# Two entries one behind the other in a hand-ordered opening stage, one transfer per unit, and copied-out pieces ahead of each block

One core of a Trainium2 chip. The metric is the device time of one execution in microseconds (us), lower is better. "Span" is the time from the first to the last instruction of one profiled execution, some 2 us less. "Granted clock" is the share of its full speed at which TensorE, the matrix engine, was allowed to run. VectorE and ScalarE work on what TensorE has left in PSUM, the memory that takes its results; POOL and SP here mostly issue transfers.

## The reference, cut to what matters

```python
# x: (8, 3136, 256); filt_r, filt_i: (1569, 256)
X = np.fft.rfft(x, axis=1)
y = np.fft.irfft(X * (filt_r + 1j * filt_i), n=3136, axis=1)   # per entry
h = y.reshape(25088, 256) @ w_in                               # 1024 columns
solu = h * softmax(h)
ln = (solu - mean(solu)) / np.sqrt(var(solu) + 1e-6) * g_ln
out = ln @ w_out
```

The transform over 3136 = 49 x 64 points is done with matrix products. One entry passes through a first stage (`pa`, eight pieces of x, results `t` stored to DRAM as `d`), a spectrum stage (`pb`, products with the filter, `pc`, results `g` stored to DRAM), and a last stage (`py`, results in `y`). Then 196 blocks of 128 rows each compute `h`, the maximum `nmax`, exp, `solu`, its square, a transposition by transfer, and `po`. The transform of the later entries is spread over the blocks of the earlier ones. The opening has nothing to hide behind: entry 0 must be through before the first block.

## The kernel before

PSUM is shared by four pools; `ps_b` has one buffer, which holds `pb` until the products have read it. "Products" are VectorE's three operations `p`, `i` and their sum; the two "turned copies" into `i` that they need are ScalarE's.

```python
GROUPS = [                       # entries, blocks of the first stage, blocks of the spectrum
    ((0, 1), None, None),        # the opening: both entries in every unit
    ((2,), (0, 6), (9, 13)),
    # ... three more groups
]
ps_h = pool("ps_h", 2, PSUM)     # h (and pa, pb in the opening)
ps_b = pool("ps_b", 1, PSUM)     # pb in the blocks
ps_t = pool("ps_t", 2, PSUM)     # pa, pc, py in the blocks
ps_o = pool("ps_o", 1, PSUM)     # po

def multiply(self, i):           # the products of a unit
    # ...
    nc.scalar.mul(turned[0:NQ], ps[NQ:P], -1.0)          # "i": ps is pb
    nc.scalar.copy(out=turned[NQ:P], in_=ps[0:NQ])
    nc.vector.tensor_tensor(out=pt, in0=ps, in1=part(0), op=ALU.mult)      # "p", the last reader of pb
    nc.vector.tensor_tensor(out=turned, in0=turned, in1=part(1), op=ALU.mult)
    nc.vector.tensor_tensor(out=pt, in0=pt, in1=turned, op=ALU.add)

# the blocks: early holds pb, half of pa and half of py; late holds pc, the other halves
with tc.manual_schedule():
    for k in range(blocks + LAG):
        if k < blocks:
            hidden(k)                           # h, nmax, exp
        if 1 <= k <= blocks:
            turn(k - 1)
        if 4 <= k < blocks + 4:
            regroup(*divmod(k - 4, 4))
        for job in early[k]:
            job()
        if k >= LAG:
            po = project(k - LAG)               # po
        if k < blocks:
            normalize(k)                        # solu, square
        if k >= LAG:
            scale(k - LAG, po)
        for job in products[k] + late[k] + stores[k] + loads[k]:
            job()
```

The opening of the kernel before is not ordered by hand; a scheduler places its instructions.

## Time and profile before

| | before |
|---|---|
| time, median of 3 runs (range) | 1904.84 us (1900.58 to 1912.51) |
| span of the profiled run, granted clock | 1902.9 us, 0.968 |
| first `h` begins | 203.42 us |
| from there to the end | 1699.5 us |
| TensorE busy, whole span | 1823.8 us |

### The profile page before, as it was taken

The numbers are of one execution on the slowest core, as the hardware profiler recorded it, in microseconds if no ns is written. First come the engines' busy times: TensorE is split into PE (matmuls) and PEld (weight loads), VectorE is DVE, ScalarE is ACT, GpSimd is POOL, SyncE is SP. The second block draws the span as 40 slices with busy tenths as digits, with TensorE's granted clock in tenths as the row PEclk, the third lists the DMA queues.
The fourth block names the chain that finished last, engine by engine and source line by source line (L and its number), as shares of the span: only waits on it lengthen the run. The fifth ranks groups of instructions, "written<-read, shape, count | busy, mean of one in ns | idle before, by whom it ended". The sixth has DMA issues, their size and how long they took to land.

```text
span 1902.9 us, 21234 instructions
## 1 busy us (share of the span) xinstructions
PE 1823.8 (96%) x6500; PEld 1168.5 (61%) x6500; DVE 1137.0 (60%) x1815; ACT 791.5 (42%) x1297; POOL 440.7 (23%) x1293
## 2 busy tenths in 40 slices
PE   6677889999999999999999999999999999999997
PEld 1224546676666666666666666667677676666665
DVE  1597445567766655566766655566666565566663
ACT  1142344554555544444545434344444334333331
POOL 2010133343334311123333211123322010110110
PEclk9686799999999999999999999999999999999999
DMA  9675279986877866575776656557675545434444
GB/s 268 214 211 188 92 226 239 241 209 174 189 194 204 200 150 149 134 170 140 166 186 148 151 137 141 137 134 177 146 178 112 119 100 117 99 86 110 96 92 100
DMA packets 320399, 300.78 MB, mean 158 GB/s; under 512 B 28625, under 2 KB 286418, under 8 KB 320288
## 3 DMA queue, kind: packets, MB, share of 16 engines
q1 hardware_dynamic: 284624, 206.69, 46.3%
q0 software_dynamic: 26704, 79.63, 14.9%
q10 hardware_dynamic: 8960, 13.11, 2.3%
q8 instruction: 53, 0.87, 0.2%
q14 instruction: 58, 0.48, 0.1%
HBM read 118.44 MB, written 81.40 MB: 105 GB/s over the span
## 4 chain that ended last, share of the span: by engine, by line
PE 88%; DVE 4%; DMA 2%; issue 1%; ACT 1%; POOL 0%; ACTq 0%; DVEq 0%; SPq 0%; POOLq 0%
PE h L396 35%; PE po L456 35%; PE py L253 6%; PE pc L226 4%; PE pb L196 4%; PE pa L169 3%; DMA d<-t 1%; DVE p L217 1%; DVE i L216 0%; DVE p L215 0%; DVE g L229 0%; DMA t<-d 0%; DVE nmax L401 0%; DMA f<-f_dram 0%; DMA raw_in<-in_moe_w_in_dram 0%
## 5 line engine op out<-in xcount | busy, mean ns | idle before, releaser
L456 PE MATMUL po<-w_out_sb,solu_t 128*128 128x256 f32 x3136 | 711.0, 380 | 4.5 <-DVE ot L464 4.5
L396 PE MATMUL h<-w_in_sb,y 128*128 128x512 f32 x1568 | 713.4, 598 | 0.0
L456 PEld LDWEIGHTS po<-w_out_sb,solu_t 128*128 128x128 f32 x3136 | 591.0, 190 | 137.7 <-issue 58.1
L396 PEld LDWEIGHTS h<-w_in_sb,y 128*128 128x128 f32 x1568 | 296.2, 192 | 317.8 <-issue 306.7
L401 DVE TENSOR_REDUCE nmax<-h 128x1 f32<-128x1024 f32 x196 | 239.6, 1222 | 419.6 <-PE h L396 419.6
L404 ACT ACTIVATE e<-h,nmax 128x1024 f32<-128x1024 f32 x196 | 218.5, 1115 | 605.0 <-DVE nmax L401 605.0
L421 ACT ACTIVATE e<-solu,nmu 128x1024 f32<-128x1024 f32 x196 | 225.0, 1148 | 287.9 <-DVE solu L419 287.9
L419 DVE SCALAR_TENSOR_TENSOR solu<-e,rsum,h 128x1024 f32<-128x1024 f32 x196 | 250.9, 1280 | 7.1 <-DVE rsum L416 0.2
L429 DVE STREAM_TRANSPOSE turn<-solu 128x1024 f32<-128x1024 f32 x196 | 241.8, 1234 | 0.0
L235 POOL DMA_DIRECT2D d<-g x152 | 93.7, 621 | 507.5 <-ACT g L229 507.4
L253 PEld LDWEIGHTS py<-wi_t,t 100*128 100x128 f32 x1024 | 146.0, 211 | 51.1 <-issue 36.0
L169 PE MATMUL pa<-x,wf_t 98*100 98x512 f32 x256 | 148.5, 687 | 25.9 <-DMA x<-in_x_dram 12.5
L253 PE MATMUL py<-wi_t,t 100*128 100x98 f32 x1024 | 145.4, 293 | 6.7 <-DMA t<-d 3.5
L448 POOL COPY rs_t<-rs 32x1 f32<-32x1 f32 x784 | 141.7, 181 | 35.7
L464 DVE TENSOR_SCALAR ot<-po,rs_t 128x256 f32<-128x256 f32 x196 | 94.4, 482 | 80.5 <-PE po L456 74.2
L215 DVE TENSOR_TENSOR p<-pb,f 128x512 f32<-128x512 f32 (+1 forms) x101 | 69.0, 684 | 120.4 <-ACT i L208 119.3
L196 PE MATMUL pb<-t,de 128*128 128x512 f32 (+1 forms) x250 | 110.9, 544 | 19.2 <-DVE p L215 10.0
L226 PE MATMUL pc<-p,de 128*128 128x512 f32 (+1 forms) x250 | 110.0, 539 | 14.9 <-DVE p L217 11.5
L442 POOL TENSOR_SCALAR rs<-var 128x4 f32<-128x4 f32 x49 | 9.3, 189 | 445.7 <-ACT e L421 443.6
L169 PEld LDWEIGHTS pa<-x,wf_t 98*100 98x100 f32 x256 | 45.7, 188 | 94.5 <-issue 59.9
L196 PEld LDWEIGHTS pb<-t,de 128*128 128x128 f32 x250 | 47.8, 198 | 78.4 <-issue 43.5
L256 ACT COPY y<-py 128x392 f32<-128x392 f32 x112 | 93.6, 836 | 5.1 <-PE py L253 5.1
(62 smaller groups left out, 868.2 us busy)
## 6 DMA issues: line engine op xcount, KB each, us to landing
solu_t<-turn SPq DMA_DIRECT2D x784, 128.0 KB
t<-d SPq DMA_DIRECT2D x64, 400.0 KB
t<-d SPq DMA_DIRECT2D x198, 128.0 KB
x<-in_x_dram SPq DMA_DIRECT2D x64, 392.0 KB
out_dram<-ot SPq DMA_DIRECT2D x196, 128.0 KB
d<-t POOLq DMA_DIRECT2D x48, 400.0 KB, 5.6
d<-g POOLq DMA_DIRECT2D x148, 128.0 KB, 3.6
f<-f_dram POOLq DMA_DIRECT2D x104, 128.0 KB, 4.3
```

Of the source, the lines that this page charges most:

```text
L169: nc.tensor.matmul(out=ps[0:NK, j], lhsT=wf_t, rhs=self.xs[i][0:NR, 2 * u:2 * u + 2, :], start=True, stop=True)
L196: nc.tensor.matmul(out=ps[:, w * j:w * j + w, :], lhsT=de[:, s + j, 0, :], rhs=t2[:, w * j:w * j + w, :], start=True, stop=True)
L226: nc.tensor.matmul(out=ps[:, w * j:w * j + w, :], lhsT=de[:, s + j, 1, :], rhs=pt[:, w * j:w * j + w, :], start=True, stop=True)
L253: nc.tensor.matmul(out=psv[:, i, :], lhsT=t4s[e, ch][:, i, cb * P:cb * P + P], rhs=wi_t, start=True, stop=True)
L396: nc.tensor.matmul(out=h[:, half, :], lhsT=y[:, c, P * t:P * t + P], rhs=w_in_sb[:, c, 512 * half:512 * half + 512], start=(c == 0), stop= ...
L401: nc.vector.tensor_reduce(out=nmax, in_=h, axis=AX.X, op=ALU.max, negate=True)
L404: nc.scalar.activation(out=e, in_=h, func=AFT.Exp, bias=nmax, accum_out=esum)
L419: nc.vector.scalar_tensor_tensor(out=solu, in0=e, scalar=rsum, in1=hs.pop(k), op0=ALU.mult, op1=ALU.mult, accum_out=nmu)
L421: nc.scalar.activation(out=e, in_=solu, func=AFT.Square, bias=nmu, scale=-float(DFF), accum_out=variances[g][:, i:i + 1])
L429: nc.vector.transpose(out=turns[g][:, :, i, :], in_=solus.pop(k).rearrange("p (f j) -> p f j", j=32))
L448: nc.gpsimd.tensor_copy(out=rss[g][32 * i:32 * i + 32, c:c + 1], in_=rs[32 * c:32 * c + 32, i:i + 1])
L456: nc.tensor.matmul(out=ps, lhsT=solu_t[:, f, :], rhs=w_out_sb[:, f, :], start=(f == 0), stop=(f == KF - 1))
```

## The change

The intent: entries 0 and 1 no longer share units but pass one behind the other, so that entry 1's first stage hides under entry 0's spectrum and entry 0's last stage under entry 1's spectrum. All tables stay resident, a unit's load and store are one transfer each, and the order is fixed by hand. In the blocks, what is copied out of PSUM ("pieces": `pa`, `py`, and with them `pb`) is to stand ahead of `h`, so that its copies run on ScalarE before exp. The core of the diff:

```diff
 GROUPS = [
-    ((0, 1), None, None),
-    ((2,), (0, 6), (9, 13)),
-    ((3, 4), (6, 13), (22, 25)),
+    ((0,), None, None),
+    ((1,), None, None),
+    ((2,), (0, 7), (9, 13)),
+    ((3, 4), (7, 12), (22, 25)),
...
-            for p in range(2):
-                nc.sync.dma_start(out=self.t2s[i][N2 * p:N2 * p + N2, 0:cols, :],
-                                  in_=self.rows(d1[self.n], s, count, p))
+            nc.sync.dma_start(out=self.t2s[i][:, 0:cols, :],
+                              in_=self.columns(d1[self.n], s, count))
...
     with ExitStack() as st:
+        st.enter_context(tc.manual_schedule())
...
+        for sp in sps:
+            if sp.n == 1:
+                for ch in range(4):
+                    fetch_back(0, ch, pools["r"])
+            else:
+                for i in range(3):
+                    sp.fetch(i)
+            forward(sp, 0)
+            for i in range(units):
+                if sp.n == 0 and i in (1, 4):
+                    load_tables(3 + i // 4)
+                sp.multiply(i)
+                if i + 1 < units:
+                    forward(sp, i + 1)
+                if sp.n == 0:
+                    if i < NH // NCH:
+                        first(NH // NCH + i)
+                    if i in (8, 10):
+                        load_weights(i // 2 - 1)
+                elif 2 <= i < 2 + NH // NCH:
+                    for cb in range(KD):
+                        back(0, i - 2, cb, nc.scalar.copy)
+                    ...
+                sp.inverse(i, nc.vector.tensor_copy if sp.n == 0 else nc.scalar.copy)
+                sp.store(i, nc.gpsimd.dma_start)
+                ...
+                if sp.n == 1 and i % 4 == 0 and i < 12:
+                    load_weights(5 + i // 4)
...
     with tc.manual_schedule():
         for k in range(blocks + LAG):
+            for job in early[k]:
+                job()
             if k < blocks:
                 hidden(k)
             if 1 <= k <= blocks:
                 turn(k - 1)
             if 4 <= k < blocks + 4:
                 regroup(*divmod(k - 4, 4))
-            for job in early[k]:
-                job()
+            if k == 1:
+                prepare_w_out()
```

`load_tables` and `load_weights` each issue a transfer and put the VectorE work that needs it right behind it. In the first six blocks both halves of a piece go to `early`.

More of the change, by code (lines that the diff above doesn't have):

```diff
@@ L58, in dft_tables @@
     v[0, :, 0], v[1, :, 0] = 1.0, 0.0
-    wf = np.zeros((N1, 2, 2, NS, 2))
-    wi = np.zeros((2, NS, 2, N1, 2))
+    wf = np.zeros((N1, 2, NS, 2, 2))
+    wi = np.zeros((NS, 2, 2, N1, 2))
     for h in range(2):
-        wf[:, h, :, :, h] = w
-        wi[:, :, h, :, h] = v.transpose(0, 2, 1) / S
+        wf[:, h, :, :, h] = w.transpose(0, 2, 1)
+        wi[:, :, h, :, h] = v.transpose(2, 0, 1) / S
     kap = np.where(q[:, None] < 32, s + N1 * q[:, None], s + N1 * (95 - q[:, None]))
@@ L108 @@
     small = pool("sm", 4)
-    d1 = [dram.tile([len(g[0]), 2 * NS, N2, C], FP32, name=f"d1_{n}") for n, g in enumerate(GROUPS)]
-    d2 = [dram.tile([len(g[0]), 2 * NS, N2, C], FP32, name=f"d2_{n}") for n, g in enumerate(GROUPS)]
+    d1 = [dram.tile([len(g[0]), NS, P, C], FP32, name=f"d1_{n}") for n, g in enumerate(GROUPS)]
+    d2 = [dram.tile([len(g[0]), NS, P, C], FP32, name=f"d2_{n}") for n, g in enumerate(GROUPS)]
     f_dram = dram.tile([NS, NQ, 2, C], FP32, name="f_dram")
@@ L120 @@
     neg_half = consts.tile([P, 4], FP32, name="neg_half")
+    ones = consts.tile([P, P], FP32, name="ones")
+    w_bar = consts.tile([P, C], FP32, name="w_bar")
     nc.vector.memset(neg_half, -0.5)
@@ L148, in __init__, with columns @@
             self.xs, self.t1s, self.t2s, self.fs, self.prods, self.gs = {}, {}, {}, {}, {}, {}
-        def rows(self, ap, s, count, p):
+        def columns(self, ap, s, count):
             if len(self.entries) == 2:
-                return ap[:, p * NS + s, :, :].rearrange("b n c -> n b c")
-            return ap[0, p * NS + s:p * NS + s + count, :, :].rearrange("s n c -> n s c")
+                return ap[:, s, :, :].rearrange("b p c -> p b c")
+            return ap[0, s:s + count, :, :].rearrange("s p c -> p s c")
         def fetch_x(self, i):
@@ L176, in store_first @@
             b, ch = divmod(i, NH // NCH)
-            dma(out=d1[self.n][b].rearrange("a (h n) c -> (a h) n c", h=2)[
+            dma(out=d1[self.n][b].rearrange("s (a n) c -> (s a) n c", a=4)[
                 :, NCH * ch:NCH * ch + NCH, :], in_=self.t1s.pop(i))
@@ L233, in store @@
             gt, cols = self.gs.pop(i), len(self.entries) * count
-            for p in range(2):
-                dma(out=self.rows(d2[self.n], s, count, p),
-                    in_=gt[N2 * p:N2 * p + N2, 0:cols, :])
+            dma(out=self.columns(d2[self.n], s, count), in_=gt[:, 0:cols, :])
     t4s = {}
@@ L245, in fetch_back @@
             out=t4s[e, ch],
-            in_=d2[n][b].rearrange("a (h n) c -> (a h) n c", h=2)[:, NCH * ch:NCH * ch + NCH, :])
+            in_=d2[n][b].rearrange("s (a n) c -> (s a) n c", a=4)[:, NCH * ch:NCH * ch + NCH, :])
     def back(e, ch, cb, evac):
@@ L256, in back, with psum @@
         evac(out=y[:, cb, t0:t0 + S].rearrange("p (r n) -> p n r", n=NH)[:, n0:n0 + NCH, :], in_=psv)
-    flip = [0]
-    def either(out, in_):
-        flip[0] ^= 1
-        if flip[0]:
-            nc.scalar.copy(out=out, in_=in_)
-        else:
-            nc.vector.tensor_copy(out=out, in_=in_)
+    def psum(kind, name):
+        return {"b": ps_b, "t": ps_t, "o": ps_o}[kind].tile([P, 2, C], FP32, name=name, tag=kind)
     with ExitStack() as st:
+        st.enter_context(tc.manual_schedule())
         pools = {name: pool(name + "0", bufs, stack=st)
-                 for name, bufs in (("r", 6), ("t1", 4), ("t2", 5), ("p", 2), ("g", 3))}
-        fpool = pool("fp", 3, stack=st)
+                 for name, bufs in (("r", 5), ("t1", 3), ("t2", 4), ("p", 2), ("g", 3))}
+        fpool = pool("fp", 1, stack=st)
         wpool = pool("wp", 1, stack=st)
+        f_all = fpool.tile([P, NS, 2, C], FP32, name="f_all")
         def load_float64(dst, src, n):
@@ L298, in load_float64, with load_tables @@
             nc.vector.tensor_tensor(out=dst, in0=frac.bitcast(FP32), in1=rest, op=ALU.add)
-        groups = {}
-        def load_group(g):
+        def load_tables(g):
             gs = slice(NG * g, NG * g + NG)
             nc.gpsimd.dma_start(out=de[:, gs, :, :], in_=de_dram[:, gs, :, :])
-            groups[g] = f = fpool.tile([P, NG, 2, C], FP32, name=f"f_{g}", tag="f")
             for k, filt in enumerate((filt_r, filt_i)):
                 for half in range(2):
-                    nc.gpsimd.dma_start(out=f[32 * half:32 * half + 32, :, k, :],
+                    nc.gpsimd.dma_start(out=f_all[32 * half:32 * half + 32, gs, k, :],
@@ L309, in load_group @@
                                         in_=filter_rows(filt, half, NG * g, NG))
-                nc.vector.tensor_copy(out=f[NQ:P, :, k, :], in_=f[0:NQ, :, k, :])
-        def resident(s, count):
-            g, i = divmod(s, NG)
-            if i == 0 and 1 <= g < NS // NG - 2:
-                load_group(g + 2)
-            return groups[g][:, i:i + count]
-        sp = Spectrum(0, pools, resident)
-        for i in range(2 * NH // NCH):
-            sp.fetch_x(i)
-            sp.first(i, (0, 1), ps_h.tile([P, 2, 512], FP32, name=f"pa_0_{i}", tag="h"), either)
-            sp.store_first(i, nc.scalar.dma_start)
-            if i < 3:
-                load_group(i)
@@ L325 @@
-        nc.gpsimd.dma_start(out=wi_t, in_=wi_dram)
-        nc.gpsimd.dma_start(out=g_sb, in_=moe_g_ln.rearrange("(k p) -> p k", p=P))
-        def start(i):
-            sp.fetch(i)
-            sp.fetch_filter(i)
-            sp.forward(i, ps_h.tile([P, 2, 512], FP32, name=f"pb_0_{i}", tag="h").rearrange(
-                "p a (b c) -> p (a b) c", c=C)[:, 0:2, :])
-        start(0)
-        for i in range(NS):
-            sp.multiply(i)
-            if i + 1 < NS:
-                start(i + 1)
-            sp.inverse(i, nc.scalar.copy if i % 3 == 0 else nc.vector.tensor_copy)
-            sp.store(i, nc.scalar.dma_start)
-            if i in (6, 9, 12, 15):
-                c, half = divmod((i - 6) // 3, 2)
-                load_float64(w_in_sb[:, c, 512 * half:512 * half + 512],
-                             w_in_words[P * c:P * c + P, 512 * half:512 * half + 512], f"in{c}{half}")
@@ L345 @@
-        for h in range(4):
-            load_float64(
-                w_out_sb[:, 2 * h:2 * h + 2, :].rearrange("p k d -> p (k d)"),
-                w_out_words[256 * h:256 * h + 256].rearrange("(k p) d w -> p k d w", p=P), f"out{h}")
-        for ch in range(NH // NCH):
-            fetch_back(0, ch, pools["r"])
-            for cb in range(KD):
-                back(0, ch, cb, either)
-        ones = wpool.tile([P, P], FP32, name="ones", tag="ones")
+                nc.vector.tensor_copy(out=f_all[NQ:P, gs, k, :], in_=f_all[0:NQ, gs, k, :])
@@ new lines, in load_weights @@
+        def load_weights(j):
+            if j < 4:
+                c, half = divmod(j, 2)
+                load_float64(w_in_sb[:, c, 512 * half:512 * half + 512],
+                             w_in_words[P * c:P * c + P, 512 * half:512 * half + 512], f"in{j}")
+            else:
+                h = j - 4
+                load_float64(
+                    w_out_sb[:, 2 * h:2 * h + 2, :].rearrange("p k d -> p (k d)"),
+                    w_out_words[256 * h:256 * h + 256].rearrange("(k p) d w -> p k d w", p=P), f"out{h}")
@@ new lines, with first @@
+        sps = [Spectrum(n, pools, lambda s, count: f_all[:, s:s + count]) for n in range(2)]
+        pieces = [(sp, i) for sp in sps for i in range(NH // NCH)]
+        units = len(sps[0].units)
+        def first(n):
+            sp, i = pieces[n]
+            sp.first(i, (0, 1), ps_h.tile([P, 2, 512], FP32, name=f"pa_{sp.n}_{i}", tag="h"),
+                     nc.scalar.copy)
+            sp.store_first(i, nc.scalar.dma_start)
+            if n + 5 < len(pieces):
+                pieces[n + 5][0].fetch_x(pieces[n + 5][1])
@@ new lines, in forward @@
+        def forward(sp, i):
+            sp.fetch_filter(i)
+            sp.forward(i, psum("bo"[i % 2], f"pb_{sp.n}_{i}"))
+        for sp, i in pieces[:5]:
+            sp.fetch_x(i)
+        for n in range(NH // NCH):
+            if n % 3 == 0:
+                load_tables(n // 3)
+            first(n)
+            if n % 3 == 1:
+                load_weights(n // 3)
+            if n == 4:
+                nc.gpsimd.dma_start(out=wi_t, in_=wi_dram)
+                nc.gpsimd.dma_start(out=g_sb, in_=moe_g_ln.rearrange("(k p) -> p k", p=P))
@@ new lines @@
+        for sp in sps:
+            if sp.n == 1:
+                for ch in range(4):
+                    fetch_back(0, ch, pools["r"])
+            else:
+                for i in range(3):
[15 more added lines that the diff above has]
+                        back(0, i - 2, cb, nc.scalar.copy)
+                    if i + 2 < NH // NCH:
+                        fetch_back(0, i + 2, pools["r"])
+                sp.inverse(i, nc.vector.tensor_copy if sp.n == 0 else nc.scalar.copy)
+                sp.store(i, nc.gpsimd.dma_start)
+                if i + 3 < units:
+                    sp.fetch(i + 3)
+                elif sp.n == 0:
+                    sps[1].fetch(i + 3 - units)
+                if sp.n == 1 and i % 4 == 0 and i < 12:
+                    load_weights(5 + i // 4)
@@ L357, with prepare_w_out @@
+    def prepare_w_out():
         nc.vector.memset(ones, 1.0)
@@ L361 @@
                                     op1=ALU.mult)
-        ps = ps_o.tile([P, C], FP32, name="ps_mean", tag="o")
+        ps = psum("o", "ps_mean")[:, 0, :]
         for f in range(KF):
@@ L365 @@
                              start=(f == 0), stop=(f == KF - 1))
-        w_bar = wpool.tile([P, C], FP32, name="w_bar", tag="w_bar")
         nc.scalar.mul(w_bar, ps, 1.0 / DFF)
@@ L452, in project @@
         g, a = divmod(k, 4)
-        ps = ps_o.tile([P, C], FP32, name=f"po_{k}", tag="o")
+        ps = ps_o.tile([P, 2, C], FP32, name=f"po_{k}", tag="o")[:, 0, :]
         solu_t = solu_ts.pop((g, a))
@@ L491 @@
     row_loads = []
-    def psum(kind, name):
-        return (ps_b if kind == "b" else ps_t).tile([P, 2, C], FP32, name=name, tag=kind)
-    for n in range(1, len(GROUPS)):
+    for n in range(2, len(GROUPS)):
         entries, first_at, spectrum_at = GROUPS[n]
@@ L502 @@
             for u in range(2):
-                (early, late)[u][t].append(lambda sp=sp, i=i, u=u: sp.first(
+                (early if t < LAG else (early, late)[u])[t].append(lambda sp=sp, i=i, u=u: sp.first(
                     i, (u,), psum("t", f"pa_{sp.n}_{i}_{u}").rearrange("p a c -> p (a c)").rearrange(
@@ L519 @@
             for cb in range(KD):
-                (early, late)[cb][t].append(
+                (early if t < LAG else (early, late)[cb])[t].append(
                     lambda e=e, ch=ch, cb=cb: back(e, ch, cb, nc.scalar.copy))
```

## The prediction

> **What bounds the kernel now.** I read the page first (busy shares, the 40 slices, the chain), then busy time by stretch, then the timeline of the opening stage, then the groups kept apart by shape.
>
> ```profile
> PE 1823.8 (96%) x6500; PEld 1168.5 (61%) x6500; DVE 1137.0 (60%) x1815; ACT 791.5 (42%) x1297; POOL 440.7 (23%) x1293
> PEclk9686799999999999999999999999999999999999
> DMA  9675279986877866575776656557675545434444
> ```
>
> TensorE is the bound, except in the first five slices or so (47 us each), where neither its clock nor its busy share is full. The table by stretch sharpens this (columns: stretch, length, then PE, PEld, DVE, ACT, POOL busy, granted clock, DMA share, GB/s):
>
> ```profile
> 0.00:50.00 50.00, 33.19 (x44) 9.40 (x44) 9.46 (x11) 6.34 (x6) 12.49 (x24) 0.91 0.92 269
> 50.00:100.00 50.00, 34.06 (x46) 10.88 (x46) 29.75 (x50) 11.82 (x18) 3.39 (x6) 0.65 0.65 212
> 100.00:150.00 50.00, 36.00 (x62) 11.30 (x62) 47.72 (x82) 21.06 (x36) 3.60 (x6) 0.90 0.67 195
> 150.00:200.00 50.00, 38.19 (x136) 29.39 (x137) 30.25 (x60) 10.51 (x15) 2.14 (x3) 0.60 0.49 161
> 700.00:1000.00 300.00, 300.00 (x1116) 196.18 (x1115) 188.16 (x296) 138.00 (x226) 76.32 (x220) 1.00 0.67 159
> ```
>
> 0 to 50 is bound by transfers (92%, 269 GB/s), 100 to 150 by VectorE (47.7 of 50), 150 to 200 by nothing that is full: work follows itself at a low clock. From 350 on TensorE is full. Matmul records at full clock last 0.4325 us for 512 columns (eight of `h` in 3.46 us), 0.216 for 256 (sixteen of `po` in 3.46) and 0.108 for `py` (eight in 0.86). By the counts of the groups: h 1568 x 0.4325 = 678, po 3136 x 0.216 = 678, pa 256 x 0.4325 = 111, py 1024 x 0.108 = 111, pb and pc together 2 x (150 x 0.4325 + 100 x 0.216) = 173; with the mean sum 1754 us. The first `h` stands here:
>
> ```profile
> 203.42 4.98 PE L396 MATMUL h<-w_in_sb,y 128*128 128x512 f32 x6
> ```
>
> Before it lie pa 64 x 0.4325 = 28, pb and pc 100 x 0.4325 = 43, py 128 x 0.108 = 14 and 3 of the mean: 88 us of work in 203 us. The opening loses 115 of the 149 us that the span has above 1754. So the change is judged by when the first block can begin.
>
> **What the Trainium skill says.** (1) "TensorE: Matmul & The Clock Gate", the HAM clock gate: the array runs at half clock until about 3.4 us of sustained activity, and falls back after such a window of idleness. The trace agrees: `pa` records last about 0.86 us in 55 to 64 us, 0.43 later, and the granted clock falls to 0.60 where waits abound. (2) The same page, "Architectural detail: the array is 16× 32×32": ScalarE and VectorE take their instructions strictly in order. The trace of before cannot contradict it, as its idle times each end with the wait of the next instruction. So a fixed order in which a VectorE instruction waits for a transfer stops all behind it. (3) "DMA: Bandwidth & Descriptors", Anatomy of one DMA: about 2 us fixed plus bytes over 436 GB/s for one transfer alone. Here raw_out, 512 KB, takes 3.9 us from issue to landing (the page's list), not far from the 3.2 of that formula; loads that share the engines take much longer (de, 640 KB: 18.4).
>
> **The change, part by part.** Work of TensorE hardly changes: a unit was one 512-column product for two entries, and is now two of 256 columns for one entry, 26 units instead of 25. What changes is order. Before, a scheduler filled VectorE's gaps. Now the opening is recorded by hand, and the built program's order on each engine shows exactly what waits stand where.
>
> *Phase A* (first stage of entry 0, until its first product). Before, all 16 pieces had to be stored: the first product is at 79.82. Now 8. Transfers: x 3.1, stores 3.3, five pieces of entry 1 2.0, three table groups 3 x 1.3, weights 1.5 MB: 13.8 MB at 269 GB/s is 51 us. Three weight conversions now stand ahead of the first product on VectorE (ten operations, about 5.3 us each), the last fetched late on the POOL queue. I take 58: a gain of 22 us.
>
> *Phase B* (spectrum of entry 0, 12.5 full units, with entry 1's first stage). One unit on VectorE is p, i, sum, then the copy of g, which must wait for pc. This loop is read from the old timeline:
>
> ```profile
> 95.42 0.68 DVE L217 TENSOR_TENSOR p<-p,i 128x512 f32<-128x512 f32 x1
> ...
> 112.10 0.68 DVE L216 TENSOR_TENSOR i<-i,f 128x512 f32<-128x512 f32 x1
> ...
> 126.09 1.13 PE L226 MATMUL pc<-p,de 128*128 128x512 f32 x2 [0.78 <-DVE p L217]
> ```
>
> Products 2.0 (0.6, 0.72, 0.69), pc with its waits 1.26, copy 0.62: 3.9; with pa's copy ahead on ScalarE 4.1. So 8 x 4.1 + 4.5 x 3.8 = 50. To this come four stops. The table groups at units 1 and 4 are issued after the previous unit's store, and VectorE's filter copies, which wait for them, stand right there, ahead of the unit's products. In the old trace filters alone took this long:
>
> ```profile
> 96.99 1.20 POOL L308 DMA_DIRECT2D f<-in_filt_r_dram  x2 [17.00 <-DVE i L216]
> 98.18 1.14 POOL L308 DMA_DIRECT2D f<-in_filt_i_dram  x2
> 103.34 0.95 DVE L310 COPY f<-f 64x1280 f32<-64x1280 f32 x1
> 107.17 0.95 DVE L310 COPY f<-f 64x1280 f32<-64x1280 f32 x1
> ```
>
> Now 640 KB of de stand ahead in the same queue: issue 1.3, some 1.2 MB at 250 GB/s 5, landing 2, the copies 2: about 10 each, 20. The conversions at units 8 and 10 wait for a load issued after the previous store: landing 5.5 after it, of which 2 lie beside the products, 5.3 of work, less what overlaps: 7 each, 14. Each stop is long enough to cool the clock: 5 in all. B is 50 + 20 + 14 + 5 and 2 to turn over to entry 1: 91.
>
> *Phase C* (spectrum of entry 1 with the last stage of entry 0, all copies on ScalarE). The chain of one unit is closed: pc 1.26, g 0.6, the two turned copies 1.2, products 2.0: 5.1 us, as p now waits for the turned copies, which stand behind g on ScalarE. 12.5 x 5.1 = 64. Three conversions: raw is issued after g's store, so the next p starts at 1.9 + 0.6 + 4.5 + 5.3 = 12 after the sum, not 3.1: 9 each, 27. Cooling 5. C is 96. py (14 of work, before 29 us alone from 174 to 203) is hidden in it.
>
> *Turn to the blocks.* By the built program's waits, the first x load of group 2 needs the memory of the filters (now all 25 resident), so it waits for the last product i of phase C. Its piece now precedes the first block: some 4.9 us, as a load of 400 KB takes in the list of the chain (t<-d at 169.31), less pc's tail: 4. Blocks begin at 58 + 91 + 96 + 4 = 249, 46 later than before.
>
> *Blocks.* Pieces ahead of each of the first six blocks let their copies run before exp, but a third piece in one block still waits for exp, product and square of the block before (1.2 + 1.3 + 0.4 + 1.4 + 1.4 = 5.7 us), and the mean of w_out, now at block 1, puts 5.6 us on VectorE. Following the chain by hand to the end of the first `po` gives 65 us; before it was 203.4 to 272.3, 69. So 4 us back. The remaining blocks are as before.
>
> Sum: 1902.9 + 46 - 4 = 1945 of span, near 1947 measured. I shade it to 1942, as stops may overlap better than my sums.
>
> **The rivals.** (a) The intended one: the pipeline of two entries hides loads, stores and py, so the opening shrinks to its transfers, about 39 MB at 250 GB/s, 156 us: 47 us gained, 1857. For it: stages of the old opening show idle engines. Against it: VectorE alone has 49 us of busy work in B and 42 in C, 58 + 91 = 149 even without one wait, and the fixed order exposes every wait. (b) Phase gains and stops cancel: stops are 4 to 5 us shorter each, since transfers find the engines less busy (under 200 GB/s in B), and the early blocks gain their full 15: 1905 to 1915. (c) TensorE stays at half clock in phase C: a unit becomes pb 1.73 + py 3.46 + pc 2.1 = 7.3; 8 units lose 2.2 each, 1965. Against: at half clock TensorE is nearly always busy and should warm.
>
> **Range and chances.** Seven stops of 7 to 10 us, each uncertain by 2.5 and in the same direction, make 15 us; phase A 5; early blocks 8: together about 18. The limit of 2% is 1942.9, right at my figure. Range 1905 to 1970. Faster by over 2% needs the stops to vanish: 0.06; within 2% 0.45; slower 0.49.
>
> **What would show it right or wrong.** In the changed profile: first product near 58; VectorE idle 6 to 9 us twice for the filter loads and five times 3 to 7 for raw loads; a unit of 4 us in B and 5 in C; the first `h` near 253; TensorE full from some 320 on. Wrong if the first `h` comes before 215, if the filter copies wait under 4 us, or if the blocks after it take more or less than 1695 us by over 10.

## The result

| | before | after |
|---|---|---|
| time, median of 4 runs (range); before has one run more than in the table above | 1904.7 us (1900.58 to 1912.51) | 2285.38 us (2282.5 to 2289.43) |
| span, granted clock | 1902.9 us, 0.968 | 2285.2 us, 0.906 |
| blocks begin (first `h`, or the pieces now ahead of it) | 203.42 us | 276.48 us |
| from there to the end | 1699.5 us | 2008.7 us |

The ratio is 1.1994, 95% interval 1.1951 to 1.2038. Ratios here are the mean time of one kernel's runs over that of the other's of the same rounds, so not quite the ratio of the medians quoted.

The page of the kernel after: busy shares, then the slices (57 us each) with TensorE's busy tenths, granted clock and DMA.

```profile
PE 1932.0 (85%) x6600; PEld 1237.8 (54%) x6600; DVE 1119.8 (49%) x1799; ACT 811.8 (36%) x1319; POOL 421.7 (18%) x1243
PE   4354579888788888999787887999999999999998
PEclk6677789899888887999888998999999999999999
DMA  8534348675545455565454554366565745544444
```

The first five slices are emptier than before, as predicted in kind. But the slices after them are not full either, up to the 25th: TensorE is at 7 to 9 tenths there, and so is its clock. By stretch, kernel before, then after (columns as in the prediction):

```profile
1000.00:1300.00 300.00, 300.00 (x1140) 199.94 (x1140) 177.25 (x280) 130.61 (x214) 66.27 (x212) 1.00 0.62 146
```

```profile
700.00:1000.00 300.00, 257.01 (x781) 151.26 (x780) 132.38 (x209) 109.85 (x182) 59.35 (x166) 0.89 0.52 129
1000.00:1300.00 300.00, 259.01 (x866) 163.80 (x865) 147.80 (x234) 108.40 (x176) 58.01 (x176) 0.91 0.51 120
```

In the same 700 to 1000 us, 781 matmul records now fit where the table of the prediction has 1116 (not quite the same blocks, as the later start shifts them). No other engine is fuller, and the DMA share is lower: nothing is a bound by its busy time. So it is a wait. The beginning of the blocks in the timeline after:

```profile
276.48 5.76 PE L172 MATMUL pa<-x,wf_t 98*100 98x512 f32 x8 [2.92 <-DMA x<-in_x_dram]
282.08 3.60 PE L417 MATMUL h<-w_in_sb,y 128*128 128x512 f32 x8
```

Of the 382 us that the span grew, 73 lie ahead of the blocks and 309 in them. Of these 309, TensorE is idle for 183 more (203.1 in place of 20.5) and busy for 127 more (1805.6 in place of 1679.0) with much the same matmuls, at a lower clock. Which wait grew, the list of waits of TensorE and of VectorE tells (engine, line, waited for: total us, times, longest), before:

```profile
PE pb L196 <- DVE p L215: 10.0, 9, 2.0
DVE nmax L401 <- PE h L396: 419.6, 156, 10.6
```

and after:

```profile
PE pb L198 <- DVE p L217: 134.0, 45, 4.2
DVE nmax L422 <- PE h L417: 752.0, 181, 13.5
```

`pb` waits for `p`, the last reader of the one `pb` buffer, and VectorE in turn waits longer for `h`. What that looks like over one block with a spectrum unit, before (rows of other work left out):

```profile
571.77 1.02 PE L196 MATMUL pb<-t,de 128*128 128x512 f32 x2
...
576.94 3.60 PE L396 MATMUL h<-w_in_sb,y 128*128 128x512 f32 x8
...
578.80 0.69 DVE L215 TENSOR_TENSOR p<-pb,f 128x512 f32<-128x512 f32 x1 [1.97 <-ACT i L208]
...
580.38 1.02 PE L196 MATMUL pb<-t,de 128*128 128x512 f32 x2
```

and after:

```profile
605.36 2.07 PE L198 MATMUL pb<-t,de 128*128 128x512 f32 x2 [3.30 <-DVE p L217]
...
607.22 4.20 PE L417 MATMUL h<-w_in_sb,y 128*128 128x512 f32 x8
...
611.46 1.23 DVE L422 TENSOR_REDUCE nmax<-h 128x1 f32<-128x1024 f32 x1 [4.83 <-PE h L417]
...
612.77 1.11 ACT L425 ACTIVATE e<-h,nmax 128x1024 f32<-128x1024 f32 x1 [7.59 <-DVE nmax L422]
...
614.40 1.28 DVE L440 SCALAR_TENSOR_TENSOR solu<-e,rsum,h 128x1024 f32<-128x1024 f32 x1
...
615.78 1.15 ACT L442 ACTIVATE e<-solu,nmu 128x1024 f32<-128x1024 f32 x1 [1.80 <-DVE solu L440]
...
617.04 0.59 ACT L209 ACTIVATE i<-pb 64x512 f32<-64x512 f32 x1
617.65 0.58 ACT L210 COPY i<-pb 64x512 f32<-64x512 f32 x1
...
618.26 0.69 DVE L217 TENSOR_TENSOR p<-pb,f 128x512 f32<-128x512 f32 x1 [2.17 <-ACT i L210]
...
619.00 2.07 PE L198 MATMUL pb<-t,de 128*128 128x512 f32 x2 [3.27 <-DVE p L217]
```

Read the second fence downward as one chain: each row begins where the one shown before it ends. `pb` begins at 605.36 and again at 619.00: 13.64 us. Before it took 580.38 - 571.77 = 8.61 for a block with the same work. Before, the products of block k (578.80 to 579.49) ran while TensorE computed `h` of block k+1, so the buffer was free when `pb` came 0.9 us later. After, `pb` stands ahead of `h`, so `h` must wait for the products of the block before, and these stand behind exp, `solu`, square and the turned copies of that block. Two chains that had overlapped follow each other. Behind this gap TensorE also runs slower for a while: `pb` lasts 2.07 us in place of 1.02 and `h` 4.20 in place of 3.60. So of the 5.03 us that the block takes longer, 3.3 are the gap and 1.65 the slower records.

So theory W: the early `pb` closes a loop over its single buffer, 13.64 - 8.61 = 5.03 us in a full case, and 76 units in the blocks; 309 / 76 = 4.1 on average if it were all of the loss. The rival P: it is the pieces (`pa`, `py`) ahead of `h`, which delay `h` or wait for their own PSUM buffers. A third suspicion, opposite to W, is that any product ahead of `h` hurts.

### The profile page after: what moved, and what is told of

The parts are those of the page before. It is cut to its first block, busy times and chain, and to the rows that moved or that the text cites. A ratio compares the mean times of both kernels' runs of the same rounds, so it can differ in the third digit from the quotient of the medians.

```text
span 2285.2 us, 21188 instructions
## 1 busy us (share of the span) xinstructions
PE 1932.0 (85%) x6600; PEld 1237.8 (54%) x6600; DVE 1119.8 (49%) x1799; ACT 811.8 (36%) x1319; POOL 421.7 (18%) x1243
## 4 chain that ended last, share of the span: by engine, by line
PE 68%; DVE 10%; ACT 8%; issue 8%; DMA 5%; SPq 1%; POOL 1%; DVEq 0%; ACTq 0%; POOLq 0%
PE h L417 31%; PE po L477 21%; PE pb L198 5%; PE py L253 5%; PE pa L172 4%; ACT e L425 3%; DVE nmax L422 3%; PE pc L228 2%; DVE p L217 2%; DVE solu L440 2%; DMA d<-t 2%; ACT i L210 2%; ACT i L209 2%; ACT e L442 1%; DMA raw_out<-in_moe_w_out_dram 1%
## 5 line engine op out<-in xcount | busy, mean ns | idle before, releaser
L417 PE MATMUL h<-w_in_sb,y 128*128 128x512 f32 x1568 | 758.1, 629 | 0.0
L417 PEld LDWEIGHTS h<-w_in_sb,y 128*128 128x128 f32 x1568 | 318.0, 207 | 361.6 <-issue 354.3
L198 PE MATMUL pb<-t,de 128*128 128x256 f32 (+1 forms) x300 | 156.3, 643 | 174.7 <-DVE p L217 134.0
L236 POOL DMA_DIRECT2D d<-g x102 | 75.6, 741 | 1039.7 <-ACT g L231 915.5
L228 PE MATMUL pc<-p,de 128*128 128x256 f32 (+1 forms) x300 | 115.0, 496 | 113.8 <-DVE p L219 113.8
L198 PEld LDWEIGHTS pb<-t,de 128*128 128x128 f32 x300 | 67.8, 248 | 217.6 <-DVE p L217 159.7
L228 PEld LDWEIGHTS pc<-p,de 128*128 128x128 f32 x300 | 60.5, 210 | 134.3 <-issue 85.5
L217 DVE TENSOR_TENSOR p<-pb,f 128x512 f32<-128x512 f32 (+1 forms) x76 | 52.0, 685 | 165.3 <-ACT i L210 165.3
L175 ACT COPY t<-pa 100x512 f32<-100x512 f32 (+1 forms) x112 | 71.2, 642 | 171.5 <-PE pa L172 114.1
L256 ACT COPY y<-py 128x392 f32<-128x392 f32 x128 | 106.2, 831 | 70.0 <-PE py L253 69.6
```

The lines of the kernel that those rows point to most:

```text
L198: nc.tensor.matmul(out=ps[:, w * j:w * j + w, :], lhsT=de[:, s + j, 0, :], rhs=t2[:, w * j:w * j + w, :], start=True, stop=True)
L228: nc.tensor.matmul(out=ps[:, w * j:w * j + w, :], lhsT=de[:, s + j, 1, :], rhs=pt[:, w * j:w * j + w, :], start=True, stop=True)
L417: nc.tensor.matmul(out=h[:, half, :], lhsT=y[:, c, P * t:P * t + P], rhs=w_in_sb[:, c, 512 * half:512 * half + 512], start=(c == 0), stop= ...
```

## The experiments

| run | time, us | ratio to before, 95% interval |
|---|---|---|
| after | 2285.38 | 1.1994 (1.1951 to 1.2038) |
| e1_early_behind | 1974.99 | 1.0356 (1.0320 to 1.0391) |
| e2_forward_behind | 2046.0 | 1.0728 (1.0693 to 1.0764) |
| e3_products_front | 2055.82 | 1.0780 (1.0728 to 1.0831) |
| e4_before_early_front | 2220.84 | 1.1645 (1.1607 to 1.1682) |
| e5_pb_products_front | 1976.22 | 1.0366 (1.0343 to 1.0388) |
| e6_filter_ahead | 1954.27 | 1.0251 (1.0226 to 1.0275) |
| e7_weights_ahead | 1918.31 | 1.0069 (1.0049 to 1.0088) |
| e8_pipelined | 1898.75 | 0.9957 (0.9940 to 0.9974) |
| e9_g_on_vector | 2024.0 | 1.0616 (1.0594 to 1.0638) |
| e10_transfers_apart | 1901.8 | 0.9965 (0.9940 to 0.9989) |
| e11_weights_truly_ahead | 1869.55 | 0.9803 (0.9787 to 0.9820) |
| e12_two_transfers | 1868.69 | 0.9809 (0.9792 to 0.9825) |

All results were correct; each run is 2 to 4 executions. e1 to e5 and e9 change the blocks. The others change the opening, each on top of the one before (e6 on e1, then e7, e8, e10, e11, e12), so all of them have the blocks of e1.

### e1: the early jobs back behind `regroup`

```diff
-            for job in early[k]:
-                job()
             if k < blocks:
                 hidden(k)
             ...
+            for job in early[k]:
+                job()
             if k == 1:
                 prepare_w_out()
```

> The changed kernel, with the early jobs of every block (pieces and the forward product pb) put back behind the block's h, as before the change; the opening stays changed. Theory W: in the blocks the 309 us are lost because pb stands ahead of h in TensorE's order and waits there for the product of the block before, which is VectorE's last work of that block (one PSUM buffer for pb). Then blocks take about 1700 us again after a start at 276.5, in all about 1980. Rival P: the pieces in front, with their copies on ScalarE, delay h; this run doesn't tell it from W, 1980 as well. Rival L (the new layout or the one transfer per unit makes fetches late in the blocks): stays near 2285.

Measured: 1974.99, so 310 us return by moving one loop. VectorE's wait for `h` is back at its old size:

```profile
DVE nmax L422 <- PE h L417: 418.9, 154, 13.6
```

All that the blocks lost comes from the place of `early`. What is left of the loss, 68 us, is the opening.

### e4: the kernel before with its early jobs ahead of `h`

```diff
         for k in range(blocks + LAG):
+            for job in early[k]:
+                job()
             if k < blocks:
                 hidden(k)
             ...
-            for job in early[k]:
-                job()
```

> The kernel before, with one edit: the early jobs stand ahead of h in every block. Theory W: the loss of 309 us belongs to this line alone and needs nothing else of the change: 1905 + 309, so 2180 to 2240. If the loss needs the new opening, layout or groups: below 1960.

Measured: 2220.84, 314 us more than before, from the same two lines in the other kernel. The wait is the same one:

```profile
PE pb L196 <- DVE p L215: 142.9, 54, 4.2
```

With e1 this is the effect in both directions. It needs nothing of the new opening.

### e2: only `pb` behind `h`, the pieces stay in front

```diff
-            early[t].append(lambda sp=sp, i=i: sp.forward(...))
+            spectra[t].append(lambda sp=sp, i=i: sp.forward(...))
...
                 regroup(*divmod(k - 4, 4))
+            for job in spectra[k]:
+                job()
```

> The changed kernel, with only the forward products pb put back behind h; the pieces stay in front. Theory W: about 1980, within 15 of the run with all early jobs behind. Rival P (pieces in front delay h): stays within 60 us of 2285.

Measured: 2046.0. Of the 310 us, 239 return with `pb` alone, and 71 do not: a miss of W as I had put it, which gave the whole to `pb`. TensorE's waits show what the pieces wait for:

```profile
PE py L253 <- ACT g L231: 20.0, 11, 4.1
PE pa L172 <- ACT g L231: 15.4, 9, 4.0
PE py L253 <- ACT t L175: 11.5, 4, 4.5
```

The pieces use the two `ps_t` buffers, together with `pc`. The copies that free them are ScalarE's, and that of `g` stands behind square. In front of `h`, a piece waits until square of the block before is done, and `h` behind it. So both W and P act, about three to one when `pb` is put back first. The other order, the pieces alone put back, was not run, so the split is that of this order; e3, below, gives 230 and 81 by another way.

### e3: the products move forward with `pb`

```diff
-            for job in early[k]:
+            for job in early[k] + products[k]:
                 job()
...
-            for job in products[k] + late[k] + stores[k] + loads[k]:
+            for job in late[k] + stores[k] + loads[k]:
                 job()
```

> The changed kernel, pb still ahead of h, but the products of the same unit are moved to stand right behind it, ahead of h, on ScalarE and VectorE too, so pb's PSUM is read while h runs. Theory W: pb of the next block no longer waits; 1970 to 2010. A rival, that pb ahead of h is bad in itself as it delays the chain h, nmax, exp, product: above 2200.

Measured: 2055.82, above the range of W alone and far below that of the rival. `pb` no longer waits for `p` (no such row among TensorE's waits); 81 us over e1 remain, about what P costs in e2.

### e5: `pb` and products in front, the pieces behind

```diff
-            for job in early[k]:
+            for job in spectra[k] + products[k]:
                 job()
             ...regroup
+            for job in early[k]:
+                job()
```

> The changed kernel, with the forward product and its products ahead of h, and the pieces (first and last stage) behind the turning of solu as in the kernel before. Two costs were seen so far: pb ahead of h waits for products that stand at the block's end (about 240 us by the runs), and pieces ahead of h wait for PSUM buffers whose copies stand behind square on ScalarE (about 70 us). If these two are all, this kernel has neither: 1975 to 1995 us, beside the 1975 of the kernel with everything put back, and no pb row among the waits of TensorE. If a pb ahead of h is bad in itself (because products ahead of h and exp delay the block's own chain), it stays at 2040 or more.

Measured: 1976.22, the same as e1, and TensorE's waits have no row of `pb` waiting for `p`. This decides it: `pb` ahead of `h` costs nothing if its products stand with it. Not the place of `pb` was wrong but the distance between it and the last reader of its buffer. A second buffer for `pb`, which would test the same cause from the other side, was not tried.

### e9: e3 with `g` copied by VectorE

```diff
-            late[t + 1].append(lambda sp=sp, i=i: sp.inverse(i, nc.scalar.copy))
+            late[t + 1].append(lambda sp=sp, i=i: sp.inverse(i, nc.vector.tensor_copy))
```

> The kernel with products, forward product and pieces in front of h (2056 us), and one change: g, the result of the inverse product, is copied out of PSUM by VectorE and no longer by ScalarE, so it does not stand behind square there. If the pieces in front lose their 70 to 80 us because their two PSUM buffers come free only after square (TensorE waited 41 us for g and 15 for t), most of it returns: 1985 to 2010 us, with the rows of py and pa waiting for g of ScalarE gone. If pieces ahead of h delay the block by their mere length (about 1 us each), it stays within 10 us of 2056.

Measured: 2024.0, between the two expectations: 32 us of the 81 that e3 has over e1 come back. The wait moved with the copy:

```profile
PE pa L172 <- DVE g L231: 17.2, 5, 6.9
PE py L253 <- ACT t L175: 10.2, 4, 4.5
PE py L253 <- DVE g L231: 8.0, 6, 3.4
```

On VectorE the copy stands behind `solu`, less late than behind square but still at the block's end. That the order on the copying engine matters is shown; how the rest of P splits is not.

### e6: filter tables fetched ahead (with the blocks of e1)

```diff
-                    load_tables(3 + i // 4)          # transfer and copies, units 1 and 4
+                    fetch_tables(3 + i // 4)         # the transfers, units 1 and 4
+                if sp.n == 0 and i in (5, 9):
+                    copy_tables(3 + i // 9)          # VectorE's copies
```

> The changed kernel with the blocks put back, and the filter groups 3 and 4 split: the transfers stay at units 1 and 4, the copies on VectorE stand before units 5 and 9. The copies waited 14.8 and 12.5 us. If these stops lie on the opening's chain, the time falls by about 25 from 1975, to 1945 to 1955. If they are hidden behind transfers (the rival: the opening is bound by what it moves), it stays within 8 us of 1975.

Measured: 1954.27, 20.7 less than e1.

### e7: weights fetched ahead too

```diff
             convert(raws.pop(j), dst, f"w{j}")
+            if j >= 2:
+                fetch_weights(j + 1)                 # before: issued with its own conversion
```

> As the run with the filters fetched ahead, and each weight transfer issued right after the conversion before it, not with its own. The five waits for raw were 4.0, 4.4, 10.6, 8.2 and 7.3, sum 34.5 us. If all lie on the chain: about 1915, from the 1950 expected of the kernel with filters alone. If the conversions' own work (5.3 each on VectorE) was what lay on it, no more than 10 us are gained.

Measured: 1918.31, 36 less than e6, against 34.5 us of waits expected to go. The waits of VectorE for weight words fall from 46.5 us in e6 to 9.8. Both sets of stops lie on the opening's chain: the weights in full, the filters to about three quarters (20.7 of 27).

### e8: the unit's chain opened

```diff
                 if i + 1 < units:
                     forward(sp, i + 1)
+                    sp.turn(i + 1)                   # turned copies, ahead of the copy of g
...
-                sp.inverse(i, nc.vector.tensor_copy if sp.n == 0 else nc.scalar.copy)
+                sp.inverse(i, nc.scalar.copy)
...
+                for _ in range(2):
+                    next(work, None)                 # two operations of a conversion per unit
```

> As the run with filters and weights fetched ahead, and the closed chain of a unit opened: the turned copies of unit i+1 stand on ScalarE before the copy of g of unit i, all copies of g are on ScalarE, and the weight conversions are spread, two operations a unit. If the unit's chain (3.9 to 5.1 us) is what is left over VectorE's own work (products 2.0 and a share of conversions), the blocks begin at 165 to 185 us, not at 276, and the whole is 1865 to 1890, faster than both kernels. If transfers bound the opening (the two stages move 39 MB, 156 us at 250 GB/s), they begin at 200 or later and the whole is 1900 or more.

Measured: 1898.75, above the expected range, 0.4% under the kernel before; the first piece of the blocks stands at 207.94 us. By the start this speaks for the rival, an opening bound by transfers, and by the time for neither (e11 takes it up). But the trace shows another stop. On the POOL queue weight words are issued, and VectorE waits for these words until 14 us later:

```profile
95.86 0.73 POOL L283 DMA_DIRECT2D raw_out<-in_moe_w_out_dram  x1
```

```profile
109.87 0.43 DVE L294 TENSOR_SCALAR power_w<-raw_out 128x512 int32<-128x512 int32 x1 [15.49 <-DMA raw_out<-in_moe_w_out_dram]
```

### e10: transfers moved apart

```diff
-                if sp.n == 0 and i in (1, 4):
-                    fetch_tables(3 + i // 4)
-                if sp.n == 0 and i in (5, 9):
+                if sp.n == 0 and i in (1, 5):
+                    fetch_tables(3 + i // 5)
+                if sp.n == 0 and i in (6, 9):
...
-                for _ in range(2):
+                for _ in range(PACE[units * sp.n + i]):   # pauses between conversions
# and the loads of entry 0's last stage one or two per unit, not four at once
```

> The pipelined kernel (1899 us), with transfers moved apart: the second table group is fetched a unit later and behind the weight words, each conversion begins two or three units after its fetch, and the loads of entry 0's last stage no longer all stand ahead of entry 1's loads in one queue. In the pipelined kernel TensorE or VectorE still waited 15.5, 4.6, 6.5 and 6.1 us for weight words and 8.9 for a load of entry 1. If these waits lie on the chain, some 25 of 41 us return: 1870 to 1882. If the transfers only wait at another place, it stays within 6 us of 1899.

Measured: 1901.8, no change, and the waits for weight words were still there (15.2 us the longest). By its wording this speaks for the second expectation, but the fault was in my edit: the generator that records a conversion issued the next transfer only when it was resumed for the next operation, right ahead of the operation that needs it. e8 has the same fault.

### e11: the same, mended

```diff
-            yield nc.vector.tensor_tensor(out=dst, in0=frac.bitcast(FP32), in1=rest, op=ALU.add)
+            nc.vector.tensor_tensor(out=dst, in0=frac.bitcast(FP32), in1=rest, op=ALU.add)
...
             if j >= 3:
                 fetch_weights(j + 1)
+            yield
```

> A mend of the last run and of the pipelined one: there each weight transfer was in fact issued just before the first operation that needs it (the record of the program resumed a step late), so both kernels waited for its full landing, 15.5, 4.6, 6.5 and 6.1 us, and moving other transfers could not help. Here the transfer is issued right after the last operation of the conversion before, two or three units ahead of its use. If these waits lie on the chain, the rows of raw_out vanish from the waits of VectorE and some 25 of 33 to 37 us return: 1872 to 1885. If transfers bound the opening anyway (the first of those waits stood in a stretch with transfers 79% busy at 267 GB/s), no more than 8 us are gained: 1890 or more.

Measured: 1869.55, 32 less than e10 and a little below the expected range: the waits lay on the chain, and transfers did not hold the opening at 200 us. Issue and first use of the same words:

```profile
77.50 0.73 POOL L286 DMA_DIRECT2D raw_out<-in_moe_w_out_dram  x1
```

```profile
98.76 0.50 DVE L297 TENSOR_SCALAR power_w<-raw_out 128x512 int32<-128x512 int32 x1
```

No wait stands behind the second row. The first pieces of the blocks:

```profile
178.46 5.34 PE L176 MATMUL pa<-x,wf_t 98*100 98x512 f32 x8 [2.01 <-DMA x<-in_x_dram]
```

98 us earlier than in the kernel after. What bounds the opening now was not tested (transfers are busy 0.79 of the stretch from 60 to 115 us). This version is 2.0% faster than the kernel before (0.9787 to 0.982), which neither reaches nor excludes a gain of over 2%.

### e12: two transfers per unit

```diff
-            nc.sync.dma_start(out=self.t2s[i][:, 0:cols, :],
-                              in_=self.columns(d1[self.n], s, count))
+            for h in (0, 64):
+                nc.sync.dma_start(out=self.t2s[i][h:h + 64, 0:cols, :],
+                                  in_=self.columns(d1[self.n], s, count)[h:h + 64])
# and the store likewise
```

> The fastest kernel so far (1870 us), with each unit's load and store split into two transfers of 64 partitions, as the kernel before has them; everything else as it is. This tells what the part 'one transfer per unit' is worth, here where the opening has few other waits. If a second issue only takes time on queues that have room (a store's issue takes about 0.74 us on the POOL queue, and each load's some 0.35 on the SP queue), it stays within 8 us of 1870. If the second issue and its own landing lie on the units' chain in the opening, 50 issues of 0.74 and 0.35 make 27 us for the opening: 1885 to 1900.

Measured: 1868.69 beside the 1869.55 of e11: the count of transfers is worth nothing measurable here. That POOL is busy 52 us longer (473.8 in place of 422.3) costs no time.

## Why the prediction was wrong

The predicted 1942 us was 343 too low. Step by step:

- **What bounds the kernel.** Right: TensorE in the blocks, the opening ahead of them. e1 has the blocks back at full rate and e11 gains only in the opening.
- **"The remaining blocks are as before."** This is the step that failed. I followed the chain by hand through the first six blocks, where I reckoned a small gain from the pieces, and took the others as unchanged. But the line that runs `early` ahead of `h` holds for all 196, and `early` contains `pb`. The prediction had named the sign of it, "if the blocks after it take more or less than 1695 us by over 10": they took 2008.7. No rival had it either. Where I had no wait there was one of 134.0 us in all, `pb` for `p`, over a buffer that the change leaves as it was. e1 and e4 show 310 and 314 us for this line alone; e2 gives 239 to `pb` and 71 to the pieces. In the order of instructions the closed loop could have been seen: `pb`, `h`, nmax, exp, `solu`, square, turned copies, `p`, and `pb` again with one buffer.
- **Phase A, 58 us.** The first product stands at 62.88: 5 more.
- **Phase B, 91 us.** Entry 1's first product stands at 171.91, so 109. The term that was too small is "about 10 each" for the filter stops:

```profile
82.72 1.94 DVE L303 COPY f_all<-f_all 64x1280 f32<-64x1280 f32 x2 [14.84 <-DMA f_all<-in_filt_r_dram]
...
110.76 0.95 DVE L303 COPY f_all<-f_all 64x1280 f32<-64x1280 f32 x1 [12.30 <-DMA f_all<-in_filt_r_dram]
```

  14.8 and 12.3 us of wait with 2 us of copies each: 31 for the two, not 20. The landing is what I mis-sized: I had 8.3 us from the first issue (1.3 + 5 + 2), and from the issue of de at 68.92 to the copies at 82.72 it was 13.8. Between 60 and 84 us 3.92 MB were moved, not the 1.2 of my sum. The weight stops were 4.0 and 4.4 of wait and 5.3 of work each, 19 and not 14, without the overlap that I had taken off. That is at most 16 of the 18. e6 and e7 show the stops on the chain: 20.7 us returned for 27 of filter waits, 36 for all five weight waits.
- **Phase C and the turn to the blocks, 100 us.** They took 276.48 - 171.91 = 104.6. The unit of 5.1 was exact where nothing stopped it (three successive `pc` at 197.96, 203.08 and 208.21), so rival (c), a unit of 7.3 at half clock throughout, is out; only the unit behind a stop came near it (`pc` at 223.70 and 230.62, 6.9 us, with records twice as long). The wait for x was 2.92 where I had 4. The three weight stops were 10.57, 8.18 and 7.29 us of wait, where I had 3 to 7.
- **First six blocks, 4 us back.** Wrong too, by little. The first `po`, before and after:

```profile
268.68 3.64 PE L456 MATMUL po<-w_out_sb,solu_t 128*128 128x256 f32 x16
```

```profile
343.88 3.62 PE L477 MATMUL po<-w_out_sb,solu_t 128*128 128x256 f32 x16
```

  In the kernel after it ends 347.5 - 276.48 = 71.0 us behind the start of the blocks, where I had 65; before it was 68.9. So the pieces in front lost 2 us and gained none; `py` waited there for the copies of `t` (4.53 us at 291.93). With the early jobs behind `h` (e1) the blocks take 1972.2 - 279.1 = 1693 us from their first piece, but one `h` runs ahead of it there, which makes some 1697 beside the 1699.5 of before.
- **Rivals.** (b), stops that cancel, fails by the same stops. (a), the intended 1857, was wrong for this order but nearly right for the idea: with loads ahead and the chain opened, e11 reaches 1870.

The loss of 381 us by steps: 239 (`pb`), 71 (pieces), 21 (filter stops), 36 (weight stops) and some 12 left in e7 over before. These are the differences from one run to the next, so that they add up proves nothing; the experiments behind each step do. Even without the failed step the prediction would have missed: e1, with everything else of the change, is at 1975, above the range, because the opening was 28 us longer than my 249. Its loss was forecast in kind only: 46 us, where 73 were measured.

## What to carry to other kernels

When an instruction that fills a single buffer moves ahead in a loop, look for the buffer's last reader: the move is free only if that reader moves too (e5), and otherwise it can chain two iterations that had overlapped (8.6 us becomes 13.6). A line moved in a loop acts on every iteration: follow the steady state around once until it closes, not only the first turns. And where one wait stops all that stands behind it on an engine (14.84 us of VectorE at 82.72), put the transfer's issue well ahead of the work that waits for it, then check in the order of the instructions that it really stands there (e8 and e10 did not; 32 us).

## What the Trainium skill lacked or had wrong

- "Perfetto Trace Analysis", Identifying Performance Opportunities, says that the same gap repeating on the engine that should be saturated can mean that SBUF or PSUM lacks room for the next tile. This case agrees (45 waits of `pb` for `p`, 134.0 us, longest 4.2), but what is lacking there is that order alone can make such gaps: the blocks have the same buffers in both kernels, and e5 removes the gap without adding a buffer.
- "TensorE: Matmul & The Clock Gate", the HAM clock gate, sets the fall to half clock at an idle window of about 3.4 us. Here shorter gaps went with it, though not every one. Two in the kernel after, each behind matmuls at full clock:

```profile
707.49 2.07 PE L198 MATMUL pb<-t,de 128*128 128x512 f32 x2 [2.41 <-DVE p L217]
...
722.16 1.13 PE L198 MATMUL pb<-t,de 128*128 128x512 f32 x2 [2.44 <-DVE p L217]
723.12 1.02 PE L172 MATMUL pa<-x,wf_t 98*100 98x512 f32 x2
723.98 3.60 PE L417 MATMUL h<-w_in_sb,y 128*128 128x512 f32 x8
```

  The first, of 2.41 us, has `pb` at twice its length behind it; the second, of 2.44, has everything at full clock. The granted clock was 0.89 to 0.91 over 600 us. So a gap below the figure was no protection here; what decides between the two was not tested. The page does tell, further down, of short idle gaps between groups of matmuls that make the clock go back and forth, but gives no length for them.
- "DMA: Bandwidth & Descriptors", Anatomy of one DMA, has a formula for one transfer (by estimate 3.2 us for 512 KB). In e8 the 512 KB of weight words took 14.0 us from issue to landing, issued on one queue behind a table group of 1.3 MB and two stores. I found no page that says how to reckon a landing with other transfers under way or ahead in the queue; it is the kind of term that I mis-sized in phase B.
